# Theta's product in one pass of 512 columns, with low parts, row sums and a first bank moved

## The chip, the cores and the metric

One core of a Trainium2 chip runs the whole program. Its engines work side by side, each through its own queue, in an order fixed when the program is built: TensorE (PE, matrix products into PSUM), VectorE (DVE), ScalarE (ACT), GpSimd (POOL), and SyncE (SP), which issues the DMAs. An instruction waits for those it depends on, and everything behind it on its engine waits too. The metric is the time of one execution on the device in microseconds; the median of the runs counts. Two runs of before lie at 548.86 and 549.30 us.

## The reference, cut to what matters

Three layers in a row, for 4 batches of 576 positions and 512 channels (8 heads of 64):

```python
# 1 sparse attention, heads 0-3 local, heads 4-7 strided; x = attn_out as (B, S, 512)
# 2 _moe_ref
theta = x @ w_theta
cos_t, sin_t = (np.cos(theta), np.sin(theta))
zr = x * cos_t
zi = x * sin_t
y = np.einsum('ts,bsd->btd', w_tok_r, zr) + np.einsum('ts,bsd->btd', w_tok_i, zi)
u = x + y
return (u + np.maximum(u @ w_ch, 0.0)).astype(np.float32)
# 3 _moe2_ref: a gate takes 2 of 4 experts per position; each expert is a causal attention
#   (q, k, v of 64 columns from x), times wo, weighted and summed
```

## The kernel before, in words

**Numbers.** Every float32 factor is split into a rounded high part and a low part (the rest), and a product is three matmuls: high by high, low by high, high by low (`mm3`, L290 to L292). So each activation that is multiplied needs a high (a cast, on ACT or DVE) and a low (a subtraction, on DVE or POOL).

**Stages.** For batch 0 the attention (`attn_pair`, four pairs of heads, three groups each) runs first. Then a loop over batches does layer 2, and the attention of batch b+1 is mixed into it as a filler for PE (`next_pair`). Layer 3 follows from some 337 us on.

**Layer 2 of a batch.** `theta(b, h)` computes half h of theta's columns (256) for five tiles of positions (four of 128, one of 64): 12 products a tile, then on DVE a rounding trick in two passes (L313, L314), then on ACT absolute value (L315), cosine and sine (L327, L328; ACT has to load its sine table before, and the Exp table before the next Exp). `rotate(b, h)` transposes x on PE (L336), multiplies it into cos and sin on DVE (L346, L352, L353) and splits the product z into high (L356 on DVE, L358 on ACT) and low (L360; DVE in batch 0, POOL later). `tokens(b, h)` is y = wtk times z, 27 products for each of 8 y tiles a batch (tile y_b_m_n, channels m, positions n), adds it to X (L375) and splits the sum into u (L384, L385). `channels(b)` is g = u times wch, 8 groups of 12 products, each ended by a relu and an addition on DVE (L397, the "gate" of `gated[b, n, m]`). channels of batch b-1 stands in batch b, behind theta's first half.

**Weights.** wth, wtk and wch come in pieces through raw buffers in X (`load64`): DMA, a cast on ACT (L141), an operation on DVE (L142), then high on ACT (L106) and low on DVE (L108). wqk, wvg and wo come through `load_split`: DMA, high on ACT (L106), low on POOL (L108). wqk and wvg are loaded in batch 3.

**What sets the order.** A scheduler in the framework orders each engine's queue when the program is built, from its own model; `tc.issue_after(x)` makes what is inside it issue after instruction x, and a pool's number of buffers sets how far ahead a tile can be made. So the text's order is only a part of what decides, and the rows of the built program are shown below.

**Attention's softmax.** In `attn_pair` the scores s go through a maximum and a subtraction on DVE (L224, L225), Exp on ACT (L227), row sums on DVE (L233), reciprocal (L235), a multiplication by it (L236; POOL after batch 0), a transpose on PE into tp (L239) and a copy to pt on ACT (L243).

## Time and profile before

| | before |
|---|---|
| median of the runs | 549.3 us |
| profiled execution | 548.84 us |
| its span | 547.1 us |
| mean granted clock of PE, of full speed | 0.982 |
| PE busy | 523.8 us |
| DVE busy | 399.3 us |
| ACT busy | 316.8 us |
| POOL busy | 195.2 us |

The span is what the trace covers; the execution's own time has 1.7 us around it. A row of the timeline has start, duration, engine, line, operation, the written tile and the read tiles, partitions and weight columns, shape; in brackets stands how long the engine sat idle before it, and what ended that. In names "<-" separates what is written from what is read. Durations of PE's products overlap, since products are pipelined; the distance of their starts is what a product takes in a row of them.

### The profile page before, as it was taken

Reading aid. Unit: us, or ns where it says so; the run is one execution under the profiler, and the core shown is the slowest. Engines: PE = TensorE matmul, PEld = TensorE weight load, DVE = VectorE, ACT = ScalarE, POOL = GpSimd, SP = SyncE. Lnnn points to the kernel's source line nnn. Section 1 sums busy time; section 2 is a strip of 40 time slices with the busy share of each in tenths; the row PEclk is TensorE's granted clock in tenths of the full one; section 3 lists DMA queues with packets and bytes.
Section 4 is the critical chain, followed back from the end, with each engine's and each line's share of the span. In section 5 each row is a group of like instructions: output and inputs, shape, how many; then the busy total and the mean of one; then the engine's idle time right before and its main releaser. Section 6 shows DMA issues by size and latency. Waiting matters only on the chain.

```text
span 547.1 us, 12352 instructions
## 1 busy us (share of the span) xinstructions
PE 523.8 (96%) x4500; PEld 499.2 (91%) x4500; DVE 399.3 (73%) x1237; ACT 316.8 (58%) x874; POOL 195.2 (36%) x280
## 2 busy tenths in 40 slices
PE   6899889999999999999999999999999999999997
PEld 5788889999999999989999999879988998999987
DVE  6979997585847567756456443699998888888972
ACT  4878965336363263452145431587788757867873
POOL 5100023230643113542006453175456443625541
PEclk9859999999999999999999999999999999999999
DMA  9857255360202131000100021000001001100112
GB/s 269 280 186 261 61 183 160 112 205 1 87 6 88 34 134 34 23 23 15 46 0 2 3 58 40 1 1 2 1 22 54 14 2 44 45 2 10 36 46 88
DMA packets 20133, 36.62 MB, mean 67 GB/s; under 512 B 2648, under 2 KB 12040, under 8 KB 20072
## 3 DMA queue, kind: packets, MB, share of 16 engines
q1 hardware_dynamic: 20072, 35.83, 20.3%
q8 instruction: 36, 0.59, 0.5%
q14 instruction: 25, 0.20, 0.1%
HBM read 31.10 MB, written 4.72 MB: 65 GB/s over the span
## 4 chain that ended last, share of the span: by engine, by line
PE 72%; DVE 15%; ACT 6%; DMA 4%; issue 3%; POOL 0%; SPq 0%; DVEq 0%; ACTq 0%; POOLq 0%
PE y L290 6%; PE y L291 6%; PE y L292 6%; PE av L267 4%; PE g L290 3%; PE g L292 3%; PE g L291 3%; PE s L203 3%; PE tp L672 3%; PE tp L239 3%; PE th L290 3%; PE th L292 3%; PE th L291 2%; PE pq L290 2%; PE s L631 2%
## 5 line engine op out<-in xcount | busy, mean ns | idle before, releaser
L290 PE MATMUL y<-wtk_hi,zhi 128*128 128x288 f32 x288 | 86.0, 300 | 1.8 <-DVE X L375 1.2
L291 PE MATMUL y<-wtk_lo,zhi 128*128 128x288 f32 x288 | 85.5, 298 | 0.0
L292 PE MATMUL y<-wtk_hi,zlo 128*128 128x288 f32 x288 | 85.5, 298 | 0.0
L236 POOL TENSOR_TENSOR p<-p,sm 128x288 f32<-128x288 f32 (+2 forms) x36 | 22.6, 634 | 135.8 <-DVE sm L235 58.7
L667 POOL TENSOR_SCALAR p<-p,sm,gt 128x256 f32<-128x256 f32 (+3 forms) x63 | 44.9, 715 | 53.7 <-DVE sm L665 25.1
L290 PEld LDWEIGHTS y<-wtk_hi,zhi 128*128 128x128 f32 x288 | 54.0, 188 | 2.5 <-DVE X L375 1.6
L291 PEld LDWEIGHTS y<-wtk_lo,zhi 128*128 128x128 f32 x288 | 54.1, 188 | 0.1
L292 PEld LDWEIGHTS y<-wtk_hi,zlo 128*128 128x128 f32 x288 | 54.0, 188 | 0.0
L360 POOL TENSOR_TENSOR zlo<-cs,zhi 128x512 fp32r<-128x512 f32 (+1 forms) x30 | 36.0, 1213 | 49.0 <-DVE zhi L356 41.3
L290 PE MATMUL th<-wth_hi,x_hi 128*128 128x256 f32 (+1 forms) x160 | 47.6, 298 | 1.3 <-DVE cs L314 0.8
L291 PE MATMUL th<-wth_lo,x_hi 128*128 128x256 f32 (+1 forms) x160 | 45.6, 286 | 0.0
L292 PE MATMUL th<-wth_hi,x_lo 128*128 128x256 f32 (+1 forms) x160 | 45.2, 287 | 0.0
L286 POOL TENSOR_TENSOR x_lo<-X,x_hi 128x576 fp32r<-128x576 f32 x20 | 29.3, 1468 | 35.5 <-DVE x_hi L284 30.2
L243 ACT COPY pt<-tp 96x384 f32<-96x384 f32 (+2 forms) x44 | 21.1, 480 | 35.0 <-PE tp L239 34.5
L290 PE MATMUL pq<-x_hi,wqk_hi 128*128 128x288 f32 x128 | 39.6, 310 | 1.3 <-DVE q L579 1.1
L203 PE MATMUL s<-k,q 128*108 128x54 f32 (+2 forms) x320 | 40.3, 266 | 0.3 <-DMA v<-in_vs 0.3
L203 PEld LDWEIGHTS s<-k,q 128*108 128x108 f32 (+1 forms) x320 | 38.5, 188 | 0.8 <-POOL q L173 0.4
L290 PE MATMUL g<-u_hi,wch_hi 128*128 128x288 f32 x128 | 38.7, 302 | 0.0
L681 DVE TENSOR_TENSOR ptlo<-tp,pthi 128x128 fp32r<-128x128 f32 (+4 forms) x80 | 37.6, 479 | 1.1 <-ACT pthi L680 0.4
L291 PE MATMUL pq<-x_lo,wqk_hi 128*128 128x288 f32 x128 | 37.9, 296 | 0.0
L292 PE MATMUL pq<-x_hi,wqk_lo 128*128 128x288 f32 x128 | 37.8, 295 | 0.0
L291 PE MATMUL g<-u_lo,wch_hi 128*128 128x288 f32 x128 | 37.8, 295 | 0.0
(183 smaller groups left out, 1703.6 us busy)
## 6 DMA issues: line engine op xcount, KB each, us to landing
X<-in_wtk SPq DMA_DIRECT2D x8, 575.5 KB
q<-in_ql SPq DMA_DIRECT2D x7, 576.0 KB
q<-in_qs SPq DMA_DIRECT2D x6, 594.0 KB
v<-in_vl SPq DMA_DIRECT2D x24, 144.0 KB
out_t<-X SPq DMA_DIRECT2D x20, 128.0 KB
...
```

The lines of the kernel that those rows point to most:

```text
L203: nc.tensor.matmul(s[:rm, i * kw:i * kw + w], qt[:, j0 + i, :], kt[:, k0:k0 + w], start=False, stop=i == n - 1)
L236: (nc.vector if b == 0 else nc.gpsimd).tensor_tensor(tiles(p), tiles(p), each(sm), op=ALU.mult)
L239: turned = nc.tensor.transpose(tp[:kw, i * rm:(i + 1) * rm], p[:rm, i * kw:(i + 1) * kw], ident[:rm, :rm])
L243: copy(pt[:kw, :n * rm], tp[:kw, :n * rm])
L267: last = nc.tensor.matmul(av[64 * h:64 * h + 64, c0:c0 + wi], vg[:w, i, h, :], pt[:w, i, h, :wi], start=True, stop=True)
L286: halved[name] = eng.tensor_tensor(lo, x, f(hi), op=ALU.subtract).ins
L290: nc.tensor.matmul(ps, ahi, bhi, start=first, stop=False)
L291: nc.tensor.matmul(ps, ahi, blo, start=False, stop=False)
L292: return nc.tensor.matmul(ps, alo, bhi, start=False, stop=last)
L360: halved[b, h] = eng.tensor_tensor(lo, zf, f(hi), op=ALU.subtract).ins
L667: eng.tensor_scalar(p[:w, :kn], p[:w, :kn], sm[:w, t:t + 1], gt[:w, t, e:e + 1], op0=ALU.mult, op1=ALU.mult)
L681: nc.vector.tensor_tensor(dst(ptlo), src, f(dst(pthi)), op=ALU.subtract)
```

## The change

- Theta is one pass per tile: 12 products of 512 columns into a whole PSUM bank, five tiles a batch, all at the start of the batch's layer 2. The evictions, Abs and sines are 512 wide. For the tile of 64 positions cos lies in partitions 0 to 63 and sin in 64 to 127 of one tile, and one Sin with a bias of pi/2 in the first half (`quarter`) makes both. In batches 1 to 3 there is one sine pass a batch; theta's second half no longer stands between channels and y.
- In batch 0 the pieces of wtk's first half and the rotation of tile t-1 are written between the thetas of the tiles.
- z's tiles come from the pools `act` and `zu` (6 buffers for 4), `z1` goes, `rp` has 4 buffers for 5.
- Pair 1's row sums issue after the batch's last gate instead of the fifth, and its Exp after the only sine pass; pair 3's Exp waits for no sine pass any more.
- The low parts of z in batch 3's second half, and those of wqk and wvg, go from POOL to DVE.
- The first tile of `ps2` is taken by a name only, so that V's first product gets another PSUM bank than the last g.
- The local mask has three rows for four.

The core of the diff:

```diff
-    mask_l = new_mask("mask_l", [128, 4, LK], wb)
+    mask_l = new_mask("mask_l", [128, 3, LK], wb)
...
-            split_w(hi[:, c, :], lo[:, c, :], st[:, :n])
+            split_w(hi[:, c, :], lo[:, c, :], st[:, :n], 1.0, eng)
...
-                with tc.issue_after(sins[b - 1, pair // 2]) if (b > 1 and pair % 2) else nullcontext():
+                with tc.issue_after(sins[b - 1]) if (b > 1 and pair == 1) else nullcontext():
                     power = nc.scalar.activation(p[:rm, :n * kw], p[:rm, :n * kw], AF.Exp, scale=SCALE).ins
...
-                with tc.issue_after(gated[b - 2, 1, 0]) if (b > 1 and pair == 1) else nullcontext():
+                with tc.issue_after(gated[b - 2, 1, 3]) if (b > 1 and pair == 1) else nullcontext():
                     nc.vector.tensor_reduce(sm[:rm, :n], tiles(p), axis=AX.X, op=ALU.add)
...
+    def theta(b, t):
+        if t == 0:
             xsplit[b] = split_x(b)
         xs = xsplit[b]
+        w, t0 = TW[t], 128 * t
+        th = ps1.tile([128, DM], F32, tag="s" if b == 0 and t % 2 else "acc", bufs=2, name=f"th_{b}_{t}")
+        for c in range(4):
+            turned = mm3(th[:w], xs[c][0][:, t0:t0 + w], xs[c][1][:, t0:t0 + w], wth_hi[:, c, :], wth_lo[:, c, :],
+                         c == 0, c == 3)
+        if t < 4:
+            cs = rp.tile([128, 2, DM], F32, tag="cs", name=f"cs_{b}_{t}")
+            first = turn = cs[:, 1, :]
+            size = cs[:, 0, :]
+        else:
+            cs = rp.tile([128, DM], F32, tag="cs4", bufs=1, name=f"cs_{b}_{t}")
+            first, turn, size = cs[0:64], cs[64:128], cs[0:64]
+        nc.vector.tensor_scalar_add(first, th[:w], MAGIC)
+        nc.vector.scalar_tensor_tensor(turn, first, MAGIC, th[:w], op0=ALU.subtract, op1=ALU.subtract)
+        last = nc.scalar.activation(size, turn, AF.Abs)
+        trig[t] = cs
+        if b == 0:
+            sines(b, range(t, t + 1))
+        elif t == NT - 1:
             with tc.issue_after(last.ins):
+                sines(b, range(NT))
         return turned.ins
...
+                pool, tags = (act, ("ahi", "alo")) if (b == 0) == (h == 1) else (zu, ("zuhi", "zulo"))
...
-            eng = nc.gpsimd if b > 0 else nc.vector
+            eng = nc.gpsimd if b > 0 and (b, h) != (B - 1, 1) else nc.vector
             halved[b, h] = eng.tensor_tensor(lo, zf, f(hi), op=ALU.subtract).ins
...
-    zu = ph1.enter_context(tc.tile_pool(name="zu", bufs=4))
-    rp = ph1.enter_context(tc.tile_pool(name="rp", bufs=5))
-    z1 = ph1.enter_context(tc.tile_pool(name="z1", bufs=1))
+    zu = ph1.enter_context(tc.tile_pool(name="zu", bufs=6))
+    rp = ph1.enter_context(tc.tile_pool(name="rp", bufs=4))
...
     for b in range(B):
-        theta(b, 0)
+        for t in range(NT):
+            turned = theta(b, t)
+            if b == 0:
+                with tc.issue_after(valued[0]), tc.issue_after(halved["x0_0_3"]):
+                    load64(wtk_s, wtk, (2 * t, min(2 * t + 2, 9)), 0, HALF)
+                if t > 0:
+                    rotate(b, 0, [t - 1])
         if b > 0:
             next_pair(b, 0)
             channels(b - 1)
+            rotate(b, 0)
+            next_pair(b, 1)
+            next_pair(b, 2)
         else:
-            with tc.issue_after(valued[0]), tc.issue_after(halved["x0_0_3"]):
-                load64(wtk_s, wtk, 9, 0, HALF)
-        rotate(b, 0)
-        if b > 0:
-            next_pair(b, 1)
-        turned = theta(b, 1)
-        if b > 0:
-            next_pair(b, 2)
+            rotate(b, 0, [NT - 1])
         rotate(b, 1)
...
+    ps2.tile([128, 512], F32, tag="t", name="first")
```

**DVE in batch 0**, the queue where theta's first eviction stands. In these names the batch is left out and the last number is a running one: cs_0_0 is half 0, tile 0 before, cs_0 is tile 0 after; X_62 to X_64 are the raw buffers. Before:

```order
L108 TENSOR_TENSOR wtk_lo<-X_63,wtk_hi 128x2x288
L142 SCALAR_TENSOR_TENSOR X_63<-X_62,X_63 128x2x288
L108 TENSOR_TENSOR wtk_lo<-X_63,wtk_hi 128x2x288
L313 TENSOR_SCALAR cs_0_0_617<-th_0_0_604 128x256
L142 SCALAR_TENSOR_TENSOR X_63<-X_64,X_63 128x2x288
L313 TENSOR_SCALAR cs_0_1_636<-th_0_1_623 128x256
L108 TENSOR_TENSOR wtk_lo<-X_63,wtk_hi 128x2x288
L314 SCALAR_TENSOR_TENSOR cs_0_0_617<-cs_0_0_617,th_0_0_604 128x256
L313 TENSOR_SCALAR cs_0_2_655<-th_0_2_642 128x256
L314 SCALAR_TENSOR_TENSOR cs_0_1_636<-cs_0_1_636,th_0_1_623 128x256
```

and after:

```order
L108 TENSOR_TENSOR wtk_lo<-X_63,wtk_hi 128x2x288
L142 SCALAR_TENSOR_TENSOR X_63<-X_62,X_63 128x2x288
L108 TENSOR_TENSOR wtk_lo<-X_63,wtk_hi 128x2x288
L142 SCALAR_TENSOR_TENSOR X_63<-X_64,X_63 128x2x288
L108 TENSOR_TENSOR wtk_lo<-X_63,wtk_hi 128x2x288
L142 SCALAR_TENSOR_TENSOR X_63<-X_62,X_63 128x288
L108 TENSOR_TENSOR wtk_lo<-X_63,wtk_hi 128x2x288
L316 TENSOR_SCALAR cs_0_617<-th_0_604 128x512
L108 TENSOR_TENSOR wtk_lo<-X_63,wtk_hi 128x288
L316 TENSOR_SCALAR cs_1_641<-th_1_628 128x512
```

All but the last low of wtk's first half now stands ahead of the first eviction.

**POOL in batch 1** behind theta; p_1_0 to p_1_2 are pair 1's probabilities of batch 2's attention. Before:

```order
L236 TENSOR_TENSOR p_1_0_1980<-p_1_0_1980,sm_1_0_1979 128x288
L236 TENSOR_TENSOR p_1_1_2001<-p_1_1_2001,sm_1_1_2000 128x288
L236 TENSOR_TENSOR p_1_2_2022<-p_1_2_2022,sm_1_2_2021 128x288
L360 TENSOR_TENSOR zlo_0_0_1926<-cs_0_0_1633,zhi_0_0_1925 128x512
L360 TENSOR_TENSOR zlo_0_1_1934<-cs_0_1_1650,zhi_0_1_1933 128x512
L360 TENSOR_TENSOR zlo_0_2_1942<-cs_0_2_1667,zhi_0_2_1941 128x512
L360 TENSOR_TENSOR zlo_0_3_1950<-cs_0_3_1684,zhi_0_3_1949 128x512
```

and after, where the first half's z is called zahi, zalo:

```order
L361 TENSOR_TENSOR zalo_0_0_1829<-cs_0_1537,zahi_0_0_1828 128x512
L361 TENSOR_TENSOR zalo_0_1_1837<-cs_1_1554,zahi_0_1_1836 128x512
L361 TENSOR_TENSOR zalo_0_2_1845<-cs_2_1571,zahi_0_2_1844 128x512
L236 TENSOR_TENSOR p_1_0_1883<-p_1_0_1883,sm_1_0_1882 128x288
L236 TENSOR_TENSOR p_1_1_1904<-p_1_1_1904,sm_1_1_1903 128x288
L236 TENSOR_TENSOR p_1_2_1925<-p_1_2_1925,sm_1_2_1924 128x288
L361 TENSOR_TENSOR zalo_0_3_1853<-cs_3_1588,zahi_0_3_1852 128x512
L361 TENSOR_TENSOR z8lo_0_1861<-cs_4_1605,z8hi_0_1860 128x256
```

The three p have moved from ahead of the lows to a place ahead of the fourth low.

**DVE in batch 3** at the last z tiles; wqk_st are the loaded pieces of wqk. Before, with wqk's lows on POOL:

```order
L385 TENSOR_TENSOR u_0_lo<-X_64,u_0_hi 128x288 x2
L385 TENSOR_TENSOR u_1_lo<-X_64,u_1_hi 128x288
L346 TENSOR_TENSOR cs_1_3_4036<-cs_1_3_4036,xn_1_3_4091 128x512
L375 TENSOR_TENSOR X_64<-y_1_1_4253,X_64 128x288
L352 TENSOR_TENSOR cs_1_4_4053<-xn_1_4_4099,cs_1_4_4053 64x256
L353 TENSOR_TENSOR cs_1_4_4053<-xn_1_4_4099,cs_1_4_4053 64x256
L356 CAST zhi_1_4_4102<-cs_1_4_4053 128x256
L385 TENSOR_TENSOR u_1_lo<-X_64,u_1_hi 128x288
L375 TENSOR_TENSOR X_64<-y_2_0_4294,X_64 128x288
```

and after:

```order
L348 TENSOR_TENSOR cs_3_3500<-cs_3_3500,xn_1_3_3707 128x2x256
L361 TENSOR_TENSOR zzulo_1_3_3711<-cs_3_3500,zzuhi_1_3_3710 128x512
L354 TENSOR_TENSOR cs_4_3517<-xn_1_4_3715,cs_4_3517 64x256 x2
L108 TENSOR_TENSOR wqk_lo<-wqk_st_3735,wqk_hi 128x512
L108 TENSOR_TENSOR wqk_lo<-wqk_st_3739,wqk_hi 128x512
L357 CAST z8hi_1_3718<-cs_4_3517 128x256
L108 TENSOR_TENSOR wqk_lo<-wqk_st_3743,wqk_hi 128x512
L386 TENSOR_TENSOR u_0_lo<-X_64,u_0_hi 128x288
L386 TENSOR_TENSOR u_1_lo<-X_64,u_1_hi 128x288
L386 TENSOR_TENSOR u_0_lo<-X_64,u_0_hi 128x288
L361 TENSOR_TENSOR z8lo_1_3719<-cs_4_3517,z8hi_1_3718 128x256
```

wqk's lows and the u lows now stand around the last z tile's high (z8hi) and low (z8lo).

## Rows read from the trace of the kernel before

**Rows 1.** The page: busy time of each engine; the chain that ended last, by engine.
```profile
PE 523.8 (96%) x4500; PEld 499.2 (91%) x4500; DVE 399.3 (73%) x1237; ACT 316.8 (58%) x874; POOL 195.2 (36%) x280
...
PE 72%; DVE 15%; ACT 6%; DMA 4%; issue 3%; POOL 0%; SPq 0%; DVEq 0%; ACTq 0%; POOLq 0%
```

**Rows 2.** Windows: stretch, length; PE, PEld, DVE, ACT, POOL busy; clock, DMA share, GB/s.
```profile
37.00:82.00 45.00, 40.54 (x310) 38.77 (x310) 42.60 (x95) 37.43 (x90) 3.62 (x4) 0.97 0.55 182
82.00:200.00 118.00, 117.76 (x1200) 114.75 (x1199) 80.62 (x221) 50.14 (x121) 37.02 (x42) 1.00 0.27 88
```

**Rows 3.** PE's waits: line, what it waited for, us in total, times, longest.
```profile
PE s L199 <- DVE mask_l L81: 5.0, 1, 5.0
PE tp L239 <- ACT pt L243: 2.1, 2, 1.1
...
PE pv L290 <- DVE X L397: 0.6, 1, 0.6
```

**Rows 4.** Timeline of PE: theta's products, and one of 512 columns in layer 3.
```profile
45.51 0.28 PE L290 MATMUL th<-wth_hi,x_hi 128*128 128x256 f32 x1
...
48.27 0.28 PE L292 MATMUL th<-wth_hi,x_lo 128*128 128x256 f32 x1
...
385.24 0.39 PE L632 MATMUL s<-klow,q 128*128 128x512 f32 x1
385.47 0.29 PE L290 MATMUL pq<-x_hi,wqk_hi 128*128 128x288 f32 x1
...
385.74 0.29 PE L292 MATMUL pq<-x_hi,wqk_lo 128*128 128x288 f32 x1
```

**Rows 5.** Timeline of DVE in batch 0, from theta's first eviction on.
```profile
40.99 0.42 DVE L313 TENSOR_SCALAR cs<-th 128x256 f32<-128x256 f32 x1
...
43.32 0.42 DVE L313 TENSOR_SCALAR cs<-th 128x256 f32<-128x256 f32 x1
43.65 0.41 DVE L314 SCALAR_TENSOR_TENSOR cs<-cs,th 128x256 f32<-128x256 f32 x1
44.38 0.76 DVE L108 TENSOR_TENSOR wtk_lo<-X,wtk_hi 128x576 fp32r<-128x576 f32 x1 [0.31 <-ACT wtk_hi L106]
...
46.81 0.69 DVE L346 TENSOR_TENSOR cs<-cs,xn 128x512 f32<-128x512 f32 x1 [0.65 <-ACT cs L328]
```

**Rows 6.** Groups by line and form: count, busy us, mean ns of one, idle before.
```profile
L360 POOL TENSOR_TENSOR zlo<-cs,zhi 128x512 fp32r<-128x512 f32 x24 | 31.4, 1324 | 43.5 <-DVE zhi L356 35.8 <-ACT zhi L358 4.3 <-PE xn L336 3.3
L236 POOL TENSOR_TENSOR p<-p,sm 128x288 f32<-128x288 f32 x18 | 13.1, 737 | 113.7 <-ACT u_hi L384 55.9 <-DVE sm L235 41.7 <-DVE sm L234 7.9
...
L360 DVE TENSOR_TENSOR zlo<-cs,zhi 128x512 fp32r<-128x512 f32 x8 | 5.4, 680 | 0.0
```

**Rows 7.** Timelines of ACT and PE at batch 2's second sine pass.
```profile
235.26 1.28 ACT L227 ACT_TABLE_LOAD   x1
...
237.48 0.44 PE L239 MATMUL tp<-ident,p 108*54 108x108 f32 x3 [1.08 <-ACT pt L243]
```

**Rows 8.** Timeline of ACT in batch 0: the cast of wtk's fifth piece.
```profile
43.27 0.53 ACT L141 CAST X<-X 128x288 f16<-128x288 bf16 x1 [1.95 <-DMA X<-in_wtk]
```

**Rows 9.** Timelines of DVE, ACT and PE where batch 0's weights end.
```profile
71.23 0.45 DVE L142 SCALAR_TENSOR_TENSOR X<-X,X 128x288 uint32<-128x288 uint32 x1
...
75.90 0.77 ACT L141 CAST X<-X 128x512 f16<-128x512 bf16 x1 [1.48 <-DMA X<-in_wch]
...
77.67 0.51 PE L239 MATMUL tp<-ident,p 128*96 128x128 f32 x3 [1.01 <-ACT pt L243]
```

**Rows 10.** Timelines of DVE and ACT in batch 3 at the last z tile.
```profile
310.40 0.42 DVE L352 TENSOR_TENSOR cs<-xn,cs 64x256 f32<-64x256 f32 x1 [0.71 <-PE xn L336]
...
311.45 1.66 ACT L106 ACTIVATE wqk_hi<-wqk_st 128x512 fp32r<-128x512 f32 x3
...
313.46 1.54 DVE L385 TENSOR_TENSOR u_lo<-X,u_hi 128x288 fp32r<-128x288 f32 x1 [1.89 <-ACT u_hi L384]
```

**Rows 11.** Timeline of DVE at the start: the local mask's copy.
```profile
3.56 1.20 DVE L79 COPY mask_l<-mask_l 64x96 bf16<-64x96 bf16 x1
```

More of the change, by code (lines that the diff above doesn't have):

```diff
@@ L128, in load64 @@
         n = n1 - n0
-        for c in range(0, kt, 2):
-            m = min(2, kt - c)
+        for c in range(*kt, 2):
+            m = min(2, kt[1] - c)
             place = X[3] if late or len(pieces) % 2 else X[1]
@@ L298, in fused_kernel @@
     xsplit, trig, z = {}, {}, {}
-    def theta(b, h):
-        if h == 0:
+    def theta(b, t):
+        if t == 0:
             xsplit[b] = split_x(b)
         xs = xsplit[b]
-        d0 = 256 * h
-        for t in range(NT):
-            w, t0 = TW[t], 128 * t
-            th = ps1.tile([128, 512], F32, tag="s" if b == 0 and t % 2 else "acc", bufs=2, name=f"th_{b}_{h}_{t}")
-            for c in range(4):
-                turned = mm3(th[:w, :256], xs[c][0][:, t0:t0 + w], xs[c][1][:, t0:t0 + w],
-                             wth_hi[:, c, d0:d0 + 256], wth_lo[:, c, d0:d0 + 256], c == 0, c == 3)
-            cs = rp.tile([128, 2, 256], F32, tag="cs", name=f"cs_{b}_{h}_{t}")
-            r = cs[:w, 1, :]
-            nc.vector.tensor_scalar_add(r, th[:w, :256], MAGIC)
-            nc.vector.scalar_tensor_tensor(r, r, MAGIC, th[:w, :256], op0=ALU.subtract, op1=ALU.subtract)
-            last = nc.scalar.activation(cs[:w, 0, :], r, AF.Abs)
-            trig[h, t] = cs
-            if b == 0:
-                sines(b, h, range(t, t + 1))
-        if b > 0:
+        w, t0 = TW[t], 128 * t
[17 more added lines that the diff above has]
+        elif t == NT - 1:
@@ L320, in theta, with sines @@
             with tc.issue_after(last.ins):
[L321 removed]
+                sines(b, range(NT))
         return turned.ins
[L324 removed]
+    def sines(b, tiles):
         for t in tiles:
[L326 to L332 removed]
+            cs = trig[t]
+            if t < 4:
+                nc.scalar.activation(cs[:, 0, :], cs[:, 0, :], AF.Sin, bias=halfpi, scale=-TWO_PI)
+                sins[b] = nc.scalar.activation(cs[:, 1, :], cs[:, 1, :], AF.Sin, scale=-TWO_PI).ins
+            else:
+                sins[b] = nc.scalar.activation(cs, cs, AF.Sin, bias=quarter, scale=-TWO_PI).ins
@@ L333, in rotate @@
+    def rotate(b, h, tiles=range(NT)):
+        for t in tiles:
+            w, t0, hs = TW[t], 128 * t, slice(256 * h, 256 * h + 256)
             tag, bufs = ("av", 2) if b == 0 and t % 3 else ("xn", 1)
@@ L470, in fused_kernel @@
         if b == 0:
-            with tc.issue_after(sins[0, 1]):
+            with tc.issue_after(sins[0]):
                 for n0 in range(0, DM, 256):
-                    load64(wch_s, wch, 4, n0, n0 + 256, late=True)
+                    load64(wch_s, wch, (0, 4), n0, n0 + 256, late=True)
             next_pair(b, 2)
```

54 lines of the change are left out of this document (21 added, 33 removed).

## The prediction

> **What bounds the kernel now.** I read the page's busy times and its chain first. PE is busy 523.8 of 547.1 us, 96% of the span, and the chain that ended last lies on PE for 72%, on DVE for 15% [rows 1]. So time can come only from shorter products and from PE's few waits, or be lost in new waits. The windows say where the waits are: from 37 to 82 us PE is busy 40.54 of 45 us and DVE 42.60, so PE waits there because DVE is full; from 82 to 200 us PE lacks 0.24 us of 118, and DVE has room (80.62) [rows 2]. The list of PE's waits names them: 5.0 us once at the start, for a mask; after that two waits of up to 1.1 us for ACT's pt, one of 0.6 ahead of V [rows 3]. Every term below is a microsecond or two, and they stand against each other.
>
> The sum is made against the profiled execution, 548.84 us; the median of the runs, 549.3, is 0.5 above it.
>
> **Theta in 512 columns.** Twelve products of a 128-row tile replace 24. Before, they start 120 ns apart: from 45.51 to 48.27 there are 23 steps in 2.76 us [rows 4]. The kernel has products of 128x512 elsewhere: one starts at 385.24 and the next product at 385.47, so 230 ns [rows 4]. A tile saves 24 x 120 - 12 x 230 = 120 ns; four tiles of a batch 0.48 us, the tile of 64 rows something below 0.12, taken as 0.06. That is 0.54 us a batch, **-1.6 us** for batches 1 to 3; batch 0 is worked out apart. By the Trainium skill (TensorE: Matmul & The Clock Gate, Back-to-back issue gap) the isolated gap is N/2.4 + 2.5 ns; the 192 full-tile pairs would save 2.5 ns each, 0.5 us in all batches. The rows disagree: a product shows a fixed part of 10 ns, and 192 pairs save 1.9 us.
>
> DVE's two evictions of 256 columns start 0.33 us apart and last 0.42 (43.32, 43.65 [rows 5]), so 0.09 overlap; a pass of 512 lasts 0.68 [rows 6] and should step by 0.60. Ten passes of 0.60 for twenty of 0.33 are 0.6 us less DVE work a batch. ACT loses a second sine pass with its table load of 1.28 us [rows 7]. In batches 1 to 3 neither engine is full [rows 2], so I cost both at nothing there, except at a named wait.
>
> **Batch 0, where DVE is full.** Before, DVE starts theta's first eviction at 40.99 and works the wtk pieces in between [rows 5]. After, the order puts all five pieces of wtk's first half, but for one low, ahead of it. The fifth piece is late: ACT sits idle 1.95 us for its DMA and starts its cast at 43.27 [rows 8]. DVE fills 2.0 us from 40.99 (three passes of 0.67), waits till about 43.7, does 1.1 us more, and reaches the first eviction at about 45: four passes' work done earlier, but some 1.4 us idle with the short waits. Then it evicts tiles 0 to 2 (six passes and a low, 4 us, to about 49), and has nothing until tile 0's sine: Abs on ACT from 47.2 (0.5), the table load (1.28), two sines of about 0.5 and 0.6 at 512 columns, and the slips between them, to about 50.9; 1.9 us idle. The two idle stretches of DVE at this place before are 0.31 and 0.65 [rows 5]. So DVE loses 3.3 - 1.0 = 2.3 us and gains 0.6 by wider passes; lesser waits of DVE on PE's new order I put at 0.7 (estimate). The lag can be followed to one place: before, the last wtk piece leaves its raw buffer at 71.23, the wch DMA that needs the buffer is there for ACT at 75.90, a pt stands behind this cast in ACT's queue, and PE's tp waits for it to 77.67, 1.01 us [rows 9]. With DVE 2.4 us later for the same work, and 2.7 us of attention work now ahead of it, that piece goes to about 76.4; PE has the same attention products behind it by then. I take **+2.4 us**. Bounds: below, DVE has no idle at all from 37 to 82 us, 2.4 + 0.6 = 3.0 us faster; above, the whole shift of 5.2 us reaches PE.
>
> **Batches 1 and 2: z's lows on POOL.** Before, POOL does pair 1's three p, then four z lows; after, three lows, the three p, then the fourth low. The p wait for row sums that are now issued after the last gate of the channels, not the fifth, three groups of 12 products later (0.135 each between 385.47 and 385.74 [rows 4], 1.6 us a group): 4.8 us. Let G be theta's end. The channels take 8 x 1.6 = 13 us, with transposes and pieces of attention the sums come at about G+16, the three p (0.74 each [rows 6]) end at G+18, the fourth low (1.32 [rows 6]) at G+19.2, or at G+17.9 if the sums come early. PE no longer has theta's second half (7 us) between channels and y, and reaches that low after 22 products of y and pair 1's first transposes, about G+18.7. I take +0.5 us for each of the two batches, **+1.0**; bounds 0 and 2.2 a batch, the latter if PE stands before all three p. In batch 2 a wait goes: pt stood behind a sine pass that ends in a table load at 235.26, and PE waited 1.08 us to 237.48 [rows 7], 1.2 with the broken stream. **-1.2 us**, bound 0 if that pt waits for the later sums instead.
>
> **Batch 3: lows on DVE.** POOL needs 1.32 us for a z low, DVE 0.68 [rows 6]; the wqk and wvg lows go over as well, some 6.5 us of DVE work in all, beside 73% busy [rows 1]. Capacity is there; the order costs. Two wqk lows stand ahead of the last z high, a third and three u lows ahead of the last z low. ACT makes the first three wqk highs from 311.45 in 1.66 us [rows 10]. So DVE finishes the last z high at about 313.5 and, after 0.6 + 3 x 0.37 + 0.34 of work, its low at 315.6. PE's last transpose was there at 310.40 [rows 10]; 34 y products of 0.135 later, at about 315.0, it needs that low. **+0.8 us**, and +0.4 for x's lows ahead of the fourth tile: **+1.2**; bounds -0.5 and +2.5. For the better end: a u low of 288 columns took 1.54 us at 313.46 [rows 10], beside a POOL that ran lows. The Trainium skill (SBUF — State Buffer, Who interferes with whom) says that a DVE operation with two SBUF inputs and a GpSimd one that reads SBUF exclude each other; the row agrees, and by that rule u's lows get faster in this stretch.
>
> **V's first bank, the mask.** PE waits 0.6 us for the last gate ahead of V's first product [rows 3]; another bank ends that, with the refill **-0.7**. The mask's copy on DVE takes 1.20 us at 3.56 for 96 columns [rows 11], while POOL fills q; two more memsets on POOL shift that by a tenth either way. Nothing, bound -1.1 if copy and fill come apart.
>
> **Sum.** +2.4 - 1.6 + 1.0 - 1.2 + 1.2 - 0.7 = +1.1, and 548.84 + 1.1 = **549.9 us**: no change that can be told.
>
> **Rivals.** *Batch 0 comes out ahead.* DVE's two new waits are covered, since its later lows and attention's work slip into them and PE starts y with fewer waits (it lacks 4.5 of 45 us there [rows 2]). Then batch 0 gives -2, the rest -1.3: 545.5. Against it: the fifth piece's DMA is as late as before, and DVE's total slack is 2.4 us. Chance 0.28.
>
> *The lost filler makes it slower.* Between channels and y PE had 60 products of theta while POOL worked on z; now y stands on POOL's slowest step, 1.32 us a low. It decides at whether the fourth low ends before G+18.7. If the row sums come 1.5 us later than I put them, PE waits 2.2 us in batches 1 and 2, and batch 3 gives its upper bound 2.5: +2.4 for the first two and +1.3 on top of the sum, 554.6. For it: a p before the low waits for DVE, whose queue I can't follow to a microsecond. Against: three lows are done before. Chance 0.22, of which 0.04 past 560, if the same happens to each z tile.
>
> *Wide products are far cheaper.* If 512 columns stepped by 131 ns, 192 + 48 products would save 240 x (240 - 131) ns = 26 us, 523 us. The rows show 230; chance 0.01. The same section of the Trainium skill's TensorE page states this 131 as the sustained figure.
>
> *Forecast* 0.49, its own range 547.5 to 552.
>
> **Numbers.** The range runs from the first rival to the second, 545.0 to 554.5. Faster by more than 2% (11 us, about what a measurement of this kernel tells from no change) needs the third rival or gains that no row shows: 0.02. Slower 0.04, within 0.94.
>
> **What would show it.** Theta products 230 ns apart; DVE idle near 43 and 50 us and the last wch piece at ACT past 80; PE waiting half a microsecond for a POOL low in y's fourth piece in batches 1 and 2, nowhere for a pt behind a second sine pass; a wait for the last z low in batch 3; none ahead of V. I am wrong if DVE is not idle around 43 to 51 us, if PE never waits for POOL's lows, or if a single new wait is above 3 us.

## The result, and the profile after

The change makes the kernel slower by a little: 553.87 us against 549.08 (medians of four runs each; of before's four, one took 2792.86 us, the others 548.66 to 549.30). The recorded ratio is 1.0095 with a 95% interval of 1.0071 to 1.0118; the two medians alone give 1.0087. That is 4.8 us by the medians and 5.2 by the ratio, within 2%. The time is inside the range of the prediction and 4.0 us above its point. The profiled execution after has a span of 551.2 us against 547.1, so 4.1 us of the difference can be followed in the traces. Its mean granted clock is 0.982, as before.

The page of the kernel after (busy us of each engine, share of the span, instructions; then the chain that ended last, by engine):

```profile
PE 524.2 (95%) x4260; PEld 483.6 (88%) x4260; DVE 401.3 (73%) x1210; ACT 300.5 (55%) x806; POOL 181.2 (33%) x269
...
PE 72%; DVE 14%; ACT 7%; DMA 2%; issue 2%; POOL 0%; ACTq 0%; DVEq 0%; POOLq 0%
```

Beside [rows 1], PE has 240 products fewer and is busy for as long; the chain is PE's for the same 72%. The page alone tells nothing more. So I cut the span by PE's own landmarks: theta's first product of batch 0, the last y product of each batch (y0 to y3), V's first product (pv). The times are starts of PE rows, in us.

| stage | before | after | difference | the prediction's terms |
|---|---|---|---|---|
| start to theta of batch 0 | 36.14 | 35.96 | -0.2 | 0 |
| theta to y0 | 67.39 | 68.62 | +1.2 | +2.4 |
| y0 to y1 | 82.66 | 82.38 | -0.3 | -0.54 + 0.5 = 0.0 |
| y1 to y2 | 78.99 | 78.04 | -1.0 | -0.54 + 0.5 - 1.2 = -1.2 |
| y2 to y3 | 58.70 | 63.09 | **+4.4** | -0.54 + 1.2 = +0.7 |
| y3 to V's first product | 13.57 | 13.57 | 0.0 | -0.7 |
| V's first product to the end | 209.60 | 209.54 | -0.1 | 0 |

Everything but batch 3 comes out within 1.2 us of its term. Batch 3 alone is 3.7 us off, and that is about the whole miss (4.0 us by the medians, 3.0 between the two profiled executions).

The list of PE's waits after (line, what it waited for, us in total, times, longest) beside [rows 3]:

```profile
PE s L199 <- DVE mask_l L81: 6.0, 1, 6.0
PE y L290 <- DVE X L376: 2.3, 2, 1.8
...
PE y L292 <- DVE z8lo L361: 0.7, 1, 0.7
...
PE pv L290 <- DVE X L398: 0.6, 1, 0.6
```

The 1.1 us for pt of the second sine pass is gone, as forecast. The wait for z8lo was forecast. The one of 1.8 us for X, the sum x + y, was not, and the one ahead of V should have gone.

**Batch 3 in the trace.** PE in the kernel after (start, duration, engine, line, operation, tiles; in brackets the idle time before it and what ended it):

```profile
317.09 0.53 PE L292 MATMUL y<-wtk_hi,z8lo 128*128 128x288 f32 x2 [0.67 <-DVE z8lo L361]
319.41 0.40 PE L290 MATMUL y<-wtk_hi,zzuhi 128*128 128x288 f32 x1 [1.79 <-DVE X L376]
```

The second wait is for a PSUM bank that the addition of an earlier y tile has to empty first. DVE in front of that addition, ACT and SP:

```profile
313.49 1.29 DVE L108 TENSOR_TENSOR wqk_lo<-wqk_st,wqk_hi 128x512 fp32r<-128x512 f32 x2 [0.59 <-ACT wqk_hi L106]
...
316.62 0.41 DVE L361 TENSOR_TENSOR z8lo<-cs,z8hi 128x256 fp32r<-128x256 f32 x1
...
317.95 0.69 DVE L108 TENSOR_TENSOR wqk_lo<-wqk_st,wqk_hi 128x512 fp32r<-128x512 f32 x1 [0.55 <-ACT wqk_hi L106]
318.56 0.42 DVE L108 TENSOR_TENSOR wvg_lo<-wvg_st,wvg_hi 128x260 fp32r<-128x260 f32 x1
318.90 0.81 DVE L376 TENSOR_TENSOR X<-y,X 128x288 f32<-128x288 f32 x2
```

```profile
314.21 0.33 SPq L117 DMA_DIRECT2D wqk_st<-in_wqk  x1
...
317.29 0.63 ACT L106 ACTIVATE wqk_hi<-wqk_st 128x512 fp32r<-128x512 f32 x1 [1.47 <-DMA wqk_st<-in_wqk]
```

These rows are one chain. wqk's pieces go through three staging buffers. The first is free when the first wqk low ends, just before 314.21, and only then can SP issue the fourth piece's DMA. It lands 3.06 us later, ACT casts it at 317.29, DVE makes its low at 317.95 and one of wvg at 318.56, and only then come the two additions at 318.90. DVE had been through with the work ahead at about 317.4: it stood idle for a weight that nothing needs until layer 3, with the addition that PE waited for behind it.

The wait has a second price. Windows of the kernel after (stretch, length; busy us of PE, PEld, DVE, ACT, POOL; granted clock, DMA share, GB/s):

```profile
316.00:320.00 4.00, 1.54 (x10) 1.08 (x9) 3.45 (x9) 1.27 (x3) 0.00 (x0) 0.98 0.37 117
320.00:324.00 4.00, 4.00 (x21) 4.00 (x21) 0.91 (x3) 1.44 (x4) 0.93 (x2) 0.60 0.18 54
324.00:328.00 4.00, 4.00 (x32) 4.00 (x32) 1.30 (x4) 1.10 (x3) 0.00 (x0) 1.00 0.00 0
```

Behind the two waits the granted clock is 0.60 from 320 to 324, so for most of that stretch it was at the lower of its two levels: 21 products start where 32 start in the next 4 us. In the chain of the kernel after they step by 0.24 us from 319.95 to 323.31, and by 0.13 afterwards:

```profile
323.07 0.24 PE y L290
...
323.46 0.13 PE y L292
```

At a clock of 0.60, 4 us of PE hold 2.4 us of work, so 1.6 us are lost. In the kernel before the clock in this stretch is 1.00, and PE waits once in the whole stage:

```profile
316.71 0.40 PE L290 MATMUL y<-wtk_hi,zhi 128*128 128x288 f32 x1 [0.42 <-DVE X L375]
```
```profile
320.00:324.00 4.00, 4.00 (x32) 4.00 (x31) 0.50 (x2) 1.17 (x3) 1.36 (x3) 1.00 0.16 40
```

Summed over the stage by the distances of PE's starts, the 4.4 us are made of waits, 2.7 us for 0.4 (a third one, 0.23 us, stands at 311.48); of y's products, 31.6 us for 29.2, where 1.6 is the slow stretch; and of g and the transposes, 0.4 more; theta takes 0.7 less. What spreads y's products by the other 0.8 us the trace doesn't name.

### The profile page after: what moved, and what is told of

Its sections match the earlier page's. It is cut to its first block, busy times and chain, and to the rows that moved or that the text cites. A ratio compares the mean times of both kernels' runs of the same rounds, so it can differ in the third digit from the quotient of the medians.

```text
span 551.2 us, 11731 instructions
## 1 busy us (share of the span) xinstructions
PE 524.2 (95%) x4260; PEld 483.6 (88%) x4260; DVE 401.3 (73%) x1210; ACT 300.5 (55%) x806; POOL 181.2 (33%) x269
## 3 DMA queue, kind: packets, MB, share of 16 engines
q1 hardware_dynamic: 20072, 35.83, 20.1%
## 4 chain that ended last, share of the span: by engine, by line
PE 72%; DVE 14%; ACT 7%; DMA 2%; issue 2%; POOL 0%; ACTq 0%; DVEq 0%; POOLq 0%
PE y L290 6%; PE y L292 5%; PE y L291 5%; PE s L203 4%; PE av L267 4%; PE g L290 3%; PE g L292 3%; PE tp L678 3%; PE g L291 3%; PE tp L239 3%; PE th L290 3%; PE th L292 3%; PE th L291 3%; PE pq L290 2%; PE s L637 2%
## 5 line engine op out<-in xcount | busy, mean ns | idle before, releaser
L290 PE MATMUL y<-wtk_hi,zzuhi 128*128 128x288 f32 x128 | 38.9, 306 | 4.0 <-DVE X L376 2.3
L291 PE MATMUL y<-wtk_lo,zzuhi 128*128 128x288 f32 x128 | 38.8, 304 | 0.6 <-DVE wtk_lo L108 0.5
L292 PE MATMUL y<-wtk_hi,zzulo 128*128 128x288 f32 x128 | 38.7, 305 | 0.5 <-DVE zzulo L361 0.5
L290 PE MATMUL y<-wtk_hi,zahi 128*128 128x288 f32 x128 | 38.9, 305 | 0.3
L361 POOL TENSOR_TENSOR zalo<-cs,zahi 128x512 fp32r<-128x512 f32 x12 | 15.5, 1300 | 69.3 <-DVE zahi L357 52.6
L292 PE MATMUL y<-wtk_hi,zalo 128*128 128x288 f32 x128 | 38.2, 300 | 0.0
L291 PE MATMUL y<-wtk_lo,zahi 128*128 128x288 f32 x128 | 38.0, 297 | 0.0
L292 PE MATMUL g<-u_hi,wch_lo 128*128 128x288 f32 x128 | 37.8, 295 | 0.0
L678 PE MATMUL tp<-ident,p 128*128 128x128 f32 (+1 forms) x240 | 36.4, 265 | 0.6 <-DVE ptlo L687 0.6
L686 ACT CAST pthi<-tp 128x128 fp32r<-128x128 f32 (+4 forms) x80 | 32.8, 425 | 7.5 <-PE tp L678 6.5
```

The source lines that it names most:

```text
L290: nc.tensor.matmul(ps, ahi, bhi, start=first, stop=False)
L291: nc.tensor.matmul(ps, ahi, blo, start=False, stop=False)
L292: return nc.tensor.matmul(ps, alo, bhi, start=False, stop=last)
L678: nc.tensor.transpose(tp[:, c * w:(c + 1) * w], p[:w, 128 * c:128 * c + 128], ident[:w, :w])
L686: nc.scalar.copy(dst(pthi), src)
```

## The experiments

**Theory**: the lows of wqk and wvg on DVE, ahead of y's additions, make batch 3's loss. **Rivals**: z's low on DVE does; or the lost filler does (theta's second half no longer stands between channels and y, so that PE is at y's last tiles too early, whoever makes the lows).

**The weights' lows alone in the kernel before.**

```diff
-            split_w(hi[:, c, :], lo[:, c, :], st[:, :n])
+            split_w(hi[:, c, :], lo[:, c, :], st[:, :n], 1.0, nc.gpsimd if name == "wo" else nc.vector)
```

> The kernel before with the lows of wqk and wvg on DVE, and nothing else. Theory: the same block appears in a kernel that has nothing else of the change, 551 to 553.5 us, with a PE wait for X of over 1 us near 317 us. Rival, the block needs the changed order of batch 3: 549 us.

551.36 us against 548.05, ratio 1.0059 (1.0041 to 1.0078): 3.3 us of loss. From y2 to batch 3's last channel product ahead of its y it takes 20.78 us (20.76 before), from there to y3 41.28 (37.94): all of it lies behind those products. PE, ACT and DVE in this run, at the last tiles of y:

```profile
317.36 0.40 PE L290 MATMUL y<-wtk_hi,zhi 128*128 128x288 f32 x1 [2.26 <-DVE X L375]
```
```profile
314.90 0.63 ACT L106 ACTIVATE wqk_hi<-wqk_st 128x512 fp32r<-128x512 f32 x1 [2.66 <-DMA wqk_st<-in_wqk]
```
```profile
315.56 0.69 DVE L108 TENSOR_TENSOR wqk_lo<-wqk_st,wqk_hi 128x512 fp32r<-128x512 f32 x1 [1.64 <-ACT wqk_hi L106]
...
316.85 0.81 DVE L375 TENSOR_TENSOR X<-y,X 128x288 f32<-128x288 f32 x2
```

It is the same chain, in a kernel that has none of the rest of the change: ACT idle for the fourth piece's DMA, DVE idle behind ACT, the additions behind both. The clock falls here too: 0.83 from 316 to 320 us and 0.75 in the next 4, which makes 1.7 us of the loss; the wait, 2.26 for 0.42, makes 1.8. This part of the change is enough for a loss of this size.

**The weights' lows back on POOL in the kernel after.**

```diff
-                    wqk_hi, wqk_lo = load_split(wc, ws, wqk, 4, 512, "wqk", nc.vector)
-                    wvg_hi, wvg_lo = load_split(wc, ws, wvg, 4, 260, "wvg", nc.vector)
+                    wqk_hi, wqk_lo = load_split(wc, ws, wqk, 4, 512, "wqk", nc.gpsimd)
+                    wvg_hi, wvg_lo = load_split(wc, ws, wvg, 4, 260, "wvg", nc.gpsimd)
```

> The changed kernel with the low parts of wqk and wvg back on POOL; z's lows of batch 3 stay on DVE. Theory: the 4.4 us that batch 3 lost come from wqk's fourth low, which stands on DVE ahead of two additions of y and waits there for a DMA; then this kernel takes about 549.5 us, PE's wait for X (1.8 us in the changed kernel) and the stretch at half clock behind it are gone. Rival, z's lows on DVE or theta's place cost it: 553 to 554 us, the wait stays.

552.9 us, 1.0093 (1.0078 to 1.0108). My expectation failed: putting them back brings nothing. PE waits 2.35 us at 319.27, for X again:

```profile
319.27 0.40 PE L290 MATMUL y<-wtk_hi,zzuhi 128*128 128x288 f32 x1 [2.35 <-DVE X L376]
```
```profile
315.10 3.02 DVE L386 TENSOR_TENSOR u_lo<-X,u_hi 128x288 fp32r<-128x288 f32 x2 [1.16 <-ACT u_hi L385]
318.04 0.81 DVE L386 TENSOR_TENSOR u_lo<-X,u_hi 128x288 fp32r<-128x288 f32 x2
318.77 0.81 DVE L376 TENSOR_TENSOR X<-y,X 128x288 f32<-128x288 f32 x2
```
```profile
313.78 4.02 POOL L108 TENSOR_TENSOR wqk_lo<-wqk_st,wqk_hi 128x512 fp32r<-128x512 f32 x3 [2.08 <-ACT wqk_hi L106]
```

The additions stand behind four u lows that took 3.76 us. The first two run beside POOL's three wqk lows (313.78 to 317.80) and take 1.58 and 1.52 us; the last two run while POOL is idle and take 0.44 and 0.45. The kernel after has three of them in 1.18 us, with POOL idle:

```profile
315.51 1.18 DVE L386 TENSOR_TENSOR u_lo<-X,u_hi 128x288 fp32r<-128x288 f32 x3
```

The Trainium skill (SBUF — State Buffer, Who interferes with whom) says that a DVE operation with two SBUF inputs and a GpSimd operation that reads SBUF exclude each other; the rows agree, with 1.5 against 0.45 us. The clock behind the wait falls as in the kernel after:

```profile
320.00:324.00 4.00, 4.00 (x21) 4.00 (x20) 0.00 (x0) 0.95 (x3) 1.63 (x4) 0.59 0.28 71
```

**z's last lows on POOL, and all lows on POOL.** In the first only the line of z is undone; the second undoes this and the weights' lows, so that every low is on the engine it had before.

```diff
-            eng = nc.gpsimd if b > 0 and (b, h) != (B - 1, 1) else nc.vector
+            eng = nc.gpsimd if b > 0 else nc.vector
```

> The changed kernel with z's lows of batch 3's second half back on POOL, wqk and wvg on DVE. Theory: the last z low's wait (0.7 us) goes, the blocked queue stays, 552.5 to 553.5 us. Rival, z's lows on DVE delay everything behind them: about 550 us.

> The changed kernel with all moved lows back on POOL: z's of batch 3, wqk's and wvg's. Theory: the engine is not the cause, the order is: POOL's wqk lows now run beside four u lows on DVE, which take 0.9 us each instead of 0.4, so it stays at 551.5 to 554 us. Rival, moving lows to DVE is the cause: 549 to 550 us.

553.65 us (1.01, 1.0082 to 1.0119) and 552.74 (1.0081, 1.0057 to 1.0105). With all lows on POOL, the waits are

```profile
314.58 0.40 PE L292 MATMUL y<-wtk_hi,zzulo 128*128 128x288 f32 x1 [1.04 <-POOL zzulo L361]
320.35 0.40 PE L290 MATMUL y<-wtk_hi,zzuhi 128*128 128x288 f32 x1 [1.28 <-DVE X L376]
```

and four u lows beside POOL's lows take 4.97 us. The stage from y2 to y3 in the profiled executions:

| order | z's last lows | weights' lows | y2 to y3 |
|---|---|---|---|
| new (after) | DVE | DVE | 63.09 |
| new | DVE | POOL | 62.74 |
| new | POOL | DVE | 61.10 |
| new | POOL | POOL | 60.76 |
| old | POOL | DVE | 62.06 |
| old (before) | POOL | POOL | 58.70 |

So with the new order no division of the lows between DVE and POOL avoids a loss of at least 2.1 us in this stage. The run with z's lows alone on POOL was profiled in the fastest of its four executions, 1.7 us below their median, so its row may be too good. It has PE's waits of 0.99 us (for zzulo, at 313.20) and 1.71 (for X, at 319.39), and the clock doesn't fall behind them:

```profile
320.00:324.00 4.00, 4.00 (x32) 4.00 (x31) 1.32 (x3) 1.44 (x4) 0.92 (x2) 1.00 0.07 23
```

That even all lows on POOL lose time speaks for the lost filler. In the kernel before, ACT makes wqk's first high 17.6 us behind the batch's first y product; with all lows on POOL in the new order it comes 18.5 us behind it, in the kernel after 20.2. The weights' work meets a PE that is 0.9 to 2.6 us further in y. That the missing filler is what shifts it is argued, not shown.

**The weights elsewhere.** If the weights' place, and not their engine, is what costs, the loss should go when they stand behind y's last additions. In the first version only wqk's fourth piece and wvg are put there, on DVE; in the second all of wqk and wvg are, on POOL. `added` holds the additions of L376. Not shown of the edits: the staging pool stays open longer, and layer 3's masks are made behind the weights, as before.

```diff
+    with tc.issue_after(added[B - 1, 0, 3]):
+        load_split(wc, ws, wqk, 4, 512, "wqk", nc.vector, range(3, 4), (wqk_hi, wqk_lo))
+        wvg_hi, wvg_lo = load_split(wc, ws, wvg, 4, 260, "wvg", nc.vector)
```

and in the second

```diff
+    with tc.issue_after(added[B - 1, 0, 3]):
+        wqk_hi, wqk_lo = load_split(wc, ws, wqk, 4, 512, "wqk", nc.gpsimd)
+        wvg_hi, wvg_lo = load_split(wc, ws, wvg, 4, 260, "wvg", nc.gpsimd)
```

> The changed kernel with all these lows still on DVE, but wqk's fourth piece and all of wvg issued after the two additions of y that stood behind them. Theory of the blocked queue: the wait for X goes as in the run before, about 550 us. Rival, it is DVE's work or its contention and not the order: 553 to 554 us.

> The changed kernel with wqk and wvg loaded as a whole only after the two additions of y (m = 2, 3, first half of the positions) of batch 3, their lows on POOL. Theory: batch 3's loss is nothing but wqk's and wvg's lows standing in the way of u's lows and of these additions (in DVE's queue, or through slowed DVE operations beside POOL); then all of it goes, no PE wait over 0.6 us from 311 to 330 us, 549 to 550 us. Rival, the new order of theta costs in batch 3 by itself: 551 us or more, a wait stays.

551.0 us (1.0053, 1.0036 to 1.007) and 550.21 against 548.21 (1.0037, 1.0026 to 1.0049). PE's waits in the first version, and the window behind them:

```profile
318.14 0.53 PE L292 MATMUL y<-wtk_hi,z8lo 128*128 128x288 f32 x2 [0.67 <-DVE z8lo L361]
319.09 0.40 PE L290 MATMUL y<-wtk_hi,zzuhi 128*128 128x288 f32 x1 [0.42 <-DVE X L376]
```
```profile
320.00:324.00 4.00, 4.00 (x33) 4.00 (x32) 1.12 (x4) 0.74 (x2) 0.00 (x0) 1.00 0.25 71
```

The wait for X falls from 1.79 to 0.42, that of before, and the clock stays at 1.00; y2 to y3 takes 60.21 us. In this version the edit does what it says: the fourth low starts at 319.32, behind the additions at 318.58.

The second version does not. The weights came early, not late:

```profile
263.69 4.01 POOL L108 TENSOR_TENSOR wqk_lo<-wqk_st,wqk_hi 128x512 fp32r<-128x512 f32 x3 [2.17 <-ACT wqk_hi L106]
```

Their loads are issued from 259 us on, their lows run from 263.69 to 274, at the end of batch 2 and the start of batch 3, and the additions that they should follow come at 317.48. In these programs `issue_after` held not all that is inside it, as its description ahead of the prediction has it, but only what stands on the engine of the named instruction: the additions are on DVE, and so were the lows of the first version, but nothing of the second. So this run, and the two below that take over its edit, show the weights some 50 us earlier than in the kernel after, and what the expectations say of late weights is not what was run.

It is still a test of the place. With all of the weights' work away from y, z8lo's wait is gone too, and y2 to y3 takes 59.35 us, 0.65 above before. That is the size that the prediction gave the stage, though the wait that it was made of is gone. Between this version and the kernel after lie 3.7 us of the stage, with z's lows still on DVE and theta where the change puts it. So most of batch 3's loss is the weights' work at the place where it meets y's last tiles. On DVE that costs in either order; on POOL it costs in the new one. Layer 3's masks, which move with the weights, are not what PE waited for: in the kernel after POOL starts on them at 322.27, behind the waits. Of the 0.65 that stays, y's products make 0.6 (29.8 us for 29.2); the cause is open.

**The clock by itself.** Fourteen products, into a bank that is free by then, are put in front of the waiting y tile; nothing reads them, so that PE works while it waits.

```diff
+                if b == B - 1 and n == 1 and m == 2:
+                    with tc.issue_after(lasty[0]):
+                        fill = ps1.tile([128, 512], F32, tag="xn", bufs=1, name="fill")
+                        stream(fill, 14, wtk_hi[:, 0, :128], wtk_hi[:, 1, :HALF])
```

> The changed kernel with 14 products of 288 columns into an unused bank, put into PE's queue ahead of the y product that waits for X near 319 us (added work whose result nobody reads, 14 x 0.133 = 1.9 us, about the length of the wait). Theory: part of the loss is the stretch at half clock behind the wait, 16 products at 0.24 us instead of 0.133; then it goes, the clock stays at full speed from 320 to 324 us, and the time falls by 1.2 to 2 us to about 552. Rival, the clock falls for another reason: 554 us or more.

552.93 us (1.0084, 1.0058 to 1.0109). The window:

```profile
320.00:324.00 4.00, 3.99 (x30) 3.75 (x29) 2.19 (x6) 1.10 (x3) 0.54 (x1) 1.00 0.24 71
```

The clock is 1.00 where it was 0.60 (one profiled execution), and the part up to y3 takes 34.27 us for 35.72, so 1.45 us less, near the 1.6 worked out above. DVE's additions are as late as before the edit; the products have only kept PE busy. In the whole run the ratio falls from 1.0095 to 1.0084 only, and the intervals are wider than either step, so the 1.45 us rest on the stage.

**Row sums and V's bank** (one run). The row sums go back to the fifth gate, and the named tile of `ps2` is left out.

```diff
-                with tc.issue_after(gated[b - 2, 1, 3]) if (b > 1 and pair == 1) else nullcontext():
+                with tc.issue_after(gated[b - 2, 1, 0]) if (b > 1 and pair == 1) else nullcontext():
...
-    ps2.tile([128, 512], F32, tag="t", name="first")
```

> The changed kernel with pair 1's row sums issued after the fifth gate again, and without the named first tile of the last PSUM pool. Two places far apart. Theory: PE's short waits at the start of y in batches 1 and 2 (0.3 and 0.5 us) change by under 0.5 us each; the wait ahead of V (0.7 us) is the same with either bank. Rival: the late sums are what brings these waits or saves a longer one, over 1 us a batch; without the named tile V waits longer.

555.12 us. From theta to y2 it takes 228.7 us (229.0 after), so the place of the row sums is worth 0.3 us at most over the two batches (2.4 us move from batch 2 into batch 1, with some of the attention's products). PE's waits change their kind: at 147.20 it now waits 0.40 us for POOL's p, at 144.71 0.46 for a gate. The wait ahead of V is 0.71 us after the last g, with or without the named tile. The 1.3 us that this run is above the kernel after lie in layer 3, where the clock fell to 0.83 from 372 to 382 us; why there is open, and one run settles nothing on it.

**Batch 0 and the start.** Two pieces of wtk go behind theta's first eviction, and `quarter` is made on ACT instead of POOL, with the weights of batch 3 as in the second version above (early, as it turned out); the second kernel has `quarter` on ACT alone.

```diff
-                with tc.issue_after(valued[0]), tc.issue_after(halved["x0_0_3"]):
+                with tc.issue_after(valued[0]), tc.issue_after(halved["x0_0_3"]), \
+                        tc.issue_after(evicted[0]) if t >= 3 else nullcontext():
...
-    nc.gpsimd.memset(quarter, 0.0)
-    nc.gpsimd.memset(quarter[:64], math.pi / 2)
+    nc.scalar.activation(quarter[64:], halfpi[64:], AF.Copy, scale=0.0)
+    nc.scalar.activation(quarter[:64], halfpi[:64], AF.Copy)
```

> The kernel with wqk and wvg loaded late on POOL, and two edits more: quarter is made by two ACT operations instead of two fills on POOL, and batch 0's last two pieces of wtk's first half issue after theta's first eviction. Theory: the first gives back 1.0 us at PE's first product (4.97 instead of 6.0 us) and part of it at theta's start; the second brings theta's first eviction 1.5 us forward and batch 0 (theta's start to y's end, 68.6 us) by 1 us. In sum 548 to 549 us, no slower than before. Rival: batch 0 is bound by DVE's amount of work, so the order gives nothing there, 549.5 us.

> The changed kernel with quarter made by two ACT operations instead of two fills on POOL, nothing else. Theory: the two fills shift POOL by 0.05 us, and with that DVE's mask copies fall behind both fills of q instead of one; without them PE starts at 5.0 us as before, 553 to 553.5 us. Rival, the shorter mask is what moves it: PE's start stays at 6.0.

549.63 us against 548.32 (1.0016, 1.0002 to 1.003), and 554.0 (1.0097, 1.0079 to 1.0115). Theta to y0 takes 68.82 us in the first, no less than after. DVE starts the first eviction 8.1 us after theta's start for 8.6, but now behind idle time that PE's theta ends, so there was little to win:

```profile
45.50 1.32 DVE L316 TENSOR_SCALAR cs<-th 128x512 f32<-128x512 f32 x2 [2.13 <-PE th L292]
```

This profile is of the slowest of twelve executions, 1.2 us above their median. The median is 1.3 us above before, for 2.0 with the weights moved alone, so a small gain is not ruled out.

`quarter` on ACT doesn't bring PE's first product forward (6.25 us in both). DVE and POOL at the start, in the kernel with `quarter` alone on ACT:

```profile
3.18 2.67 DVE L88 CAST twice<-ident 128x128 bf16<-128x128 f32 x2
```
```profile
3.61 2.10 POOL L163 MEMSET q<- 128x1188 f32 x2
```

The operation that stretches has only moved, from the mask's copy to the cast before it; both end when POOL's fills of q end. So the same was tried from the other side, in the kernel before: those two fills on ACT.

```diff
-                (nc.vector if pair == 1 else nc.gpsimd).memset(qt[:, :nq * 2 * rw], 0.0)
+                if pair == 1:
+                    nc.vector.memset(qt[:, :nq * 2 * rw], 0.0)
+                else:
+                    nc.scalar.activation(qt[:, :nq * 2 * rw], halfpi.to_broadcast([128, nq * 2 * rw]), AF.Copy, scale=0.0)
```

> The kernel before with the two fills of q (batch 0, pairs 2 and 3) as ACT operations, where ACT is idle till 8 us, instead of POOL fills. Theory: DVE's mask copies (1.2 us at 3.56 in the kernel before, 2.2 us in the changed one) wait for POOL's fills; without these they take 0.2 us, PE starts at about 3.9 us instead of 5.0 (6.0 in the changed kernel), and as far as the attention of batch 0 follows, 0.5 to 1 us is gained: 547.3 to 548 us against before of the same call. Rival: the copies wait for something else, PE starts at 5.0, the time stays.

The copy takes 0.21 us where [rows 11] has 1.20, and PE starts at 4.0 us:

```profile
3.49 0.21 DVE L79 COPY mask_l<-mask_l 64x96 bf16<-64x96 bf16 x1
```
```profile
PE s L202 <- DVE mask_l L81: 4.0, 1, 4.0
```

Yet theta starts at 37.70 (36.14 before), and the time is 549.63 against 548.4 (1.0013, 0.9999 to 1.0026). DVE's first maximum of the scores still comes 0.5 us earlier (7.03 for 7.52); where the lead goes after that isn't shown. PE's first wait alone is not what the attention of batch 0 is bound by.

**The same edit in the kernel before**, all of wqk and wvg meant to stand behind y's last additions, on POOL as they were.

```diff
+    with tc.issue_after(added[B - 1, 0, 3]):
+        wqk_hi, wqk_lo = load_split(wc, ws, wqk, 4, 512, "wqk")
+        wvg_hi, wvg_lo = load_split(wc, ws, wvg, 4, 260, "wvg")
```

> The kernel before with wqk and wvg loaded after the two additions of y in batch 3, lows on POOL as they were. Theory: before, too, u's low beside POOL's wqk low (1.54 us) is behind PE's wait for X near 317 us (0.6 us with the refill); it goes, 548.0 to 548.6 us. Rival: that wait is y's own and nothing changes, 549 us.

548.87 us against 548.32, ratio 1.0002 (0.9988 to 1.0016): nothing. Here too the weights came early: POOL's wqk lows run from 261.45 us, beside DVE's u lows of batch 2 (one of them 1.53 us) and ahead of theta's evictions. The trace shows two things that cancel. At y's last tiles the wait for X (0.42) is gone, and that part takes 37.29 us for 37.94; but at the start of the batch PE now waits for an eviction:

```profile
268.86 0.39 PE L290 MATMUL th<-wth_hi,x_hi 128*128 128x256 f32 x1 [1.49 <-DVE cs L314]
```

No version that I ran is faster than the kernel before.

## Why the prediction was right or wrong

**Theta's products: right.** In batch 3 they start 230 ns apart (48 steps from 268.02 to 279.09). The first three of the batch:

```profile
265.13 0.39 PE L290 MATMUL th<-wth_hi,x_hi 128*128 128x512 f32 x1
265.36 0.39 PE L291 MATMUL th<-wth_lo,x_hi 128*128 128x512 f32 x1
265.58 0.40 PE L292 MATMUL th<-wth_hi,x_lo 128*128 128x512 f32 x1
```

The rival of 131 ns is refuted. By the Trainium skill (TensorE: Matmul & The Clock Gate, Back-to-back issue gap) the isolated gap of 512 columns would be 512/2.4 + 2.5, an estimate of 216 ns; measured are 230, as in [rows 4], and the measurement decides.

**Batch 0: DVE's lag right, its way to PE not, the size somewhat too large.** DVE in the kernel after:

```profile
43.34 0.46 DVE L142 SCALAR_TENSOR_TENSOR X<-X,X 128x288 uint32<-128x288 uint32 x1 [0.94 <-ACT X L141]
...
44.56 0.68 DVE L316 TENSOR_SCALAR cs<-th 128x512 f32<-128x512 f32 x1
...
50.66 0.69 DVE L348 TENSOR_TENSOR cs<-cs,xn 128x512 f32<-128x512 f32 x1 [1.94 <-ACT cs L332]
```

The first eviction was put at about 45 and the idle time ahead of the rotation at 1.9 us; they came at 44.56 and 1.94. The idle time ahead of the fifth piece is 0.94, for some 1.4 with short waits. The late wch piece was followed to "about 76.4" and past 80 at ACT; two pieces reach ACT at 83.01 and 85.85. But pt's wait behind it is only 0.17 us, as PE by then had other work. So the one place to which the lag was followed did not carry it. The stage lost 1.2 us in this profile; profiles with the old batch 0 show 66.5 to 67.4 us for it, those with the new 68.5 to 69.2, so the term lies between +1.1 and +2.7, about +1.8 by their means. PE's named waits in the stage are only 0.2 us longer than before (4.65 for 4.45); most of the rest is in y's products (30.9 us for 30.1 by the distances of their starts), and why the trace does not name. The rival "batch 0 comes out ahead" is refuted.

**Batches 1 and 2: the sum right by luck, the mechanism wrong.** -1.2 us against -1.3. The second sine pass went, and its wait with it. But no wait of PE for a POOL low of y is in the list, which the prediction had named as what would prove it wrong. POOL in the kernel after, batch 1, and PE:

```profile
147.83 1.96 POOL L236 TENSOR_TENSOR p<-p,sm 128x288 f32<-128x288 f32 x3 [1.68 <-DVE sm L235]
149.75 1.28 POOL L361 TENSOR_TENSOR zalo<-cs,zahi 128x512 fp32r<-128x512 f32 x1
```
```profile
149.85 0.23 PE L199 MATMUL s<-mask_s,twice 128*108 128x162 bf16 x1 [0.33 <-DVE p L225]
...
151.09 0.40 PE L292 MATMUL y<-wtk_hi,zalo 128*128 128x288 f32 x1
```

Theta ends, and channels begins, at G = 131.7. The three p end at G+18.1 and the fourth low at G+19.3, forecast at G+18 and G+19.2. The step that failed is "about G+18.7" for PE: transposes and scores of the attention stand ahead of the product that needs this low, so that PE comes to it at G+19.4, just as it lands, and waits 0.33 us for a p on DVE on the way. Other waits, 0.5 us in each batch, took the place of the one named. Theta gave 1.1 and 0.9 us for 0.54, since before its products stand 131 and 127 ns apart on average here and not 120; the transposes of x took 0.6 and 0.5 us more, which had no term. These errors cancel.

**Batch 3: this step failed.** "+0.8 for the last z low" was right: the wait is 0.67, and 0.83 with the refill (0.97 from start to start, less one product). The prediction's own times, 315.0 and 315.6, are only 0.6 apart; it does not say what the rest is. "+0.4 for x's lows ahead of the fourth tile" didn't show as such. What failed is "Capacity is there; the order costs" worked out for the z lows alone. In the rows of the order I followed three wqk lows and the u lows up to z8lo, and stopped there. Behind z8lo stood the fourth wqk low; it needs a DMA that here could not start before the first low had freed one of three buffers, and the two additions that empty y's banks stand behind it. The upper bound of +2.5 had no price for an addition made late by a DMA, nor for a clock that falls after the wait. The term measured +4.9 (the stage's +4.4 and theta's 0.5), not +1.2. The rival "the lost filler" gave 554.6 us, 0.7 above what came, by the wrong stages: batches 1 and 2 did not wait as it says, and batch 3 lost twice what it gave. Its sum has a slip as well: from 0.5 to 2.2 us in two batches is +3.4 and not +2.4, and 554.6 comes out with 3.4 only; with the 2.4 written it is 553.6. The forecast's own range, 547.5 to 552, was missed; the time lies within the full range by luck, since its upper end is this rival's. With all lows back on POOL 2.1 us of the stage's loss remain, so something in the new order besides the engines is part of the cause. With the weights away from y all but 0.65 goes, so it is not enough alone; and the old order with the weights' lows on DVE loses 3.4 us, so it is not needed either.

**V's first bank: wrong.** The wait is 0.55 us in the list after, 0.6 in [rows 3], and PE stands still for 0.71 us behind the last g with the named tile or without:

```profile
341.66 0.39 PE L290 MATMUL pv<-wvg_hi,x_hi 128*128 128x260 f32 x1 [0.55 <-DVE X L398]
```

The term took for granted that the bank is what V waits for. By the program's text V's first product has another bank than the last g, and it still waits for the last gate. Perhaps the pool `ps2`, which takes over the banks of the pool before, can be used only when the last user of that one is done; this is argued, not shown.

**The mask: right in this profile, by luck.** PE's first product came 1.0 us later (6.0 us), since the copies take 2.26 us behind POOL's fills; theta's start didn't move in this profile (35.96). But seven other profiles with the same start have theta at 36.19 to 37.12, and three with the old start at 35.83 to 36.14: 0.7 us later on average. So nothing is too little for the start as a whole. That the mask is the cause is not shown: in the run with q's fills on ACT PE starts 1 us earlier, and theta comes at 37.70.
